# Scores by head and all transposes in two PSUM banks taken in turn, q and k transposed later in the step

## The chip, the cores and the metric

The kernel runs on one core of one Trainium2 chip. The metric is device time in microseconds of one execution: before, the median of three timed runs is 744.09 us (742.8 to 744.35).

## The reference

```python
def _attn_ref(q, k, v, n_sink, window):          # (4, 8, 768, 64): batch, heads, sequence, head_dim
    scores = np.matmul(q, k.transpose(0, 1, 3, 2)) / np.sqrt(D)
    keep = is_sink | in_window                   # key < 4, or 0 <= query - key < 128
    scores = np.where(keep, scores, -1000000000.0)
    a = np.exp(scores - np.max(scores, axis=-1, keepdims=True))
    a = a / (np.sum(a, axis=-1, keepdims=True) + 1e-09)
    return np.matmul(a, v)

def _moe_ref(x, w_in, w_out):                    # x: (3072, 512), w_in: (512, 2048), w_out: (2048, 512)
    h = x @ w_in
    sp = np.maximum(h, 0.0) + np.log1p(np.exp(-np.abs(h)))
    return (h * erf(sp)) @ w_out
```

The attention's output, heads side by side, is x of the second part.

## The kernel before

**Work.** The 3072 tokens are cut into 12 groups of 256 tokens, three groups to a batch. The attention goes in 48 steps: step s is group s // 4 and head pair s % 4. The feed-forward part of a group is 16 blocks of 128 hidden units; one attention step stands beside four of them.

**One step.** `loadqk`, `loadv` (DMAs on SP's queue) bring q, k and v. `prep` transposes two tiles of k and two of q by TensorE into one PSUM tile `tqk`, and ScalarE copies it to `kq` in SBUF (L266; in the first group of a batch a second small copy, L269, puts the sink keys beside it). `score` multiplies q by k on 64x64 pieces of the array, both heads, into `ps`. `soft` is VectorE's part: two copy_predicated that fold the window together, then four masked maxima (the CUSTOM_DVE rows), each followed by ScalarE's exp (L346). `norm` divides on VectorE. `ptrans` transposes the probabilities into `tp`, `strans` the sink columns into `ts`; ScalarE copies `tp` to `pt` (L389) and `ts` to `sp` (L424), and `sinkw` reads `ts` once more on VectorE. Two steps later `av` multiplies by v, and `xfin` copies the result to `xh`, `xl`. In steps of a batch's first group `sinks` also copies the batch's 16 sink rows of v to `sv` (L277, ScalarE), which arrive by two small DMAs of their own.

**Feed-forward.** `hid` makes h in PSUM, two blocks to a tile of 24 matmuls. `act` runs three activations r (L691 to L693) and three u (L696) on ScalarE with three VectorE operations between, then rounds to `g` (VectorE) and takes the rest on GpSimd (L705). `proj` is the output product, 12 matmuls for two blocks, into `o`; after a group two copies `ot` (L724) and two DMAs write the result.

**PSUM.** Eight banks: `ps_o` two, `ps_h` two, `ps_s` two (one tile [P, 2, 512], a bank a head, used again each step), `ps_t` two, in which `tqk`, `tp`, `ts` and `av` take turns.

**Order.** From step 15 on TensorE's order is that of a table: each piece of work has a place `a`, and all are sorted by it. Step s stands at a = 4s - 6. `av` of step s - 2 and `score` of s stand at a - 0.3 and a - 0.29, `tp` and `ts` at a + 3.01, and q and k of step s (`p`) at a - 4.28, so just behind `score` of step s - 1. The other engines' order is the scheduler's, by priorities made from the same places. One step of TensorE is thus: av, ps, tqk of the next step, 24 h, 12 o, 24 h, tp, ts, 12 o.

Of the kernel before, what the change touches and what calls it, by code (L numbers as in the profile page):

```python
# [9 lines left out]
F32 = mybir.dt.float32  # L10
# [6 lines left out]
PSUM = bass.MemoryType.PSUM  # L17
DRAM = bass.MemoryType.DRAM

P = 128  # L20
# [21 lines left out]
NE, AL = 4, 2  # L42
NW = 9
NF1 = 15

PW, EA = 256, 40
O = dict(prep=-100, norm=-100, core=-300, av=-300, load=-400, ptrans=-200, xfin=-100,
# [21 lines left out]
def kernel(  # L69
# [67 lines left out]
    def fast_path():  # L137
        with ExitStack() as st:
# [3 lines left out]
            work = st.enter_context(tc.tile_pool(name="work", bufs=2))  # L142
            ps_o = st.enter_context(tc.tile_pool(name="ps_o", bufs=2, space=PSUM))
            ps_h = st.enter_context(tc.tile_pool(name="ps_h", bufs=2, space=PSUM))
            ps_s = st.enter_context(tc.tile_pool(name="ps_s", bufs=1, space=PSUM))
            ps_t = st.enter_context(tc.tile_pool(name="ps_t", bufs=2, space=PSUM))


            ri = work.tile([P, 512], I32, tag="u", bufs=UB, name="ri")
# [97 lines left out]
            def follow(prev, ins):  # L247

                if prev is not None:
                    tc.add_manual_dep(  # L250
                        ins.ins, prev.ins.name,
                        mybir.DependencyInfo(mybir.DependencyClass.NoSync, mybir.DependencyReason.DATA), reason="order",
                    )
                return ins

            def prep(s):

                g, c = divmod(s, NPAIR)
                d = stp[s]
                tp = ps_t.tile([P, 4, P], F32, tag="t", name=f"tqk_{s}")  # L260
                for j, t in enumerate((d["k"], d["q"])):
                    for i in range(2):
                        ten.transpose(
                            out=tp[:, 2 * j + i, :], in_=t[:, i].rearrange("p h d -> p (h d)"), identity=ident
                        )
                nc.scalar.copy(kq[:, c, 1:, :P], tp)  # L266
                if g % GPB == 0:
                    x = tp[:, 0, :SW].rearrange("p (o t) -> p o t", o=1)
                    nc.scalar.copy(kq[:, c, :3, P:], x.broadcast_to([P, 3, SW]))  # L269
# [16 lines left out]
            def score(s):  # L286

                g, c = divmod(s, NPAIR)
                gb = g % GPB
                d = stp[s]  # L290
                d["pst"] = pst[:, s % RING]
                if s in (2, 3):
                    t = wpool.tile([P, 2 * DM], F32, tag="wo", name=f"pst_{s}")
                    d["pst"] = t[:, : 4 * KB].rearrange("p (i h t) -> p i h t", i=2, h=2)
                d["sum"], d["neg"] = (
                    kq[:, c, 3 + i, P : P + 4].rearrange("p (i h) -> p i h", i=2) for i in range(2)
                )

                ps, both, prev = [], None, tail.pop(s - AL, None)
                for h in range(2):  # L300
                    nm = f"ps_{s}_{h}"
                    if s in (1, 2):
                        ps.append(ps_h.tile([P, 2, GT], F32, tag="h", name=nm).rearrange("p a t -> p (a t)"))
                    else:
                        if both is None:
                            both = ps_s.tile([P, 2, 512], F32, tag="s", name=f"ps_{s}")
                        ps.append(both[:, h, :])


                d["ps"] = ps, both  # L310
                for i in range(2):
                    qt = kq[:, c, 3 + i, :]
                    kt = kq[:, c].rearrange("p n t -> p (n t)")
                    for hf, r0, n, x in ((lo, KB * i, KB + 64, X[i]), (hi, KB * i + 64, KB + 80, X[i] - 80)):
                        for h in (1, 0):
                            r = slice(64 * h, 64 * h + 64)
                            prev = follow(
                                prev,
                                ten.matmul(ps[h][hf, x : x + n], qt[r, hf], kt[r, r0 : r0 + n], start=True, stop=True),
                            )  # L320
# [31 lines left out]
            def both(s):  # L352
                return shs[s % 2].rearrange("p r t -> p (r t)")[:, :P].bitcast(F32)
# [25 lines left out]
            def ptrans(s):  # L379

                i0 = 1 if (s // NPAIR) % GPB == 0 else 0
                d = stp[s]
                pool, tag = (ps_o, "o") if s < 6 else (ps_t, "t")
                tp = pool.tile([P, 2, 2, P], F32, tag=tag, name=f"tp_{s}")
                for i in range(2):
                    for h in range(2):
                        ten.transpose(out=tp[:, h, i, :], in_=d["pst"][:, i, h, :P], identity=ident)
                pt = work.tile([P, 2, 2, P], F32, tag="pt", bufs=1, name=f"pt_{s}")
                nc.scalar.copy(pt, tp)  # L389

                uo = d["uo"] = work.tile([P, 2, 2, 2, P], F32, tag="uo", bufs=AL, name=f"uo_{s}")
                for e, sg, op, i1 in ((0, 1, ALU.is_gt, i0), (1, -1, ALU.is_ge, 0)):
                    nc.gpsimd.affine_select(  # L393
                        out=uo[:, :, i1:, e, :], in_=pt[:, :, i1:, :], pattern=[[0, 2], [0, 2 - i1], [-sg, P]],
                        compare_op=op, fill=0.0, base=0, channel_multiplier=sg,
                    )
# [18 lines left out]
            def strans(s):  # L415

                d = stp[s]
                pool, tag = (ps_o, "o") if s < 6 else (ps_t, "t")
                if s >= NW:
                    ts = d["ts"] = pool.tile([P, P], F32, tag=tag, name=f"ts_{s}")  # L420
                    ten.transpose(out=ts, in_=both(s), identity=ident)
                    sp = d["sp"] = work.tile([P, 2, P], F32R, tag="sp", bufs=AL, name=f"sp_{s}")
                    for i in range(2):
                        nc.scalar.activation(sp[:, i, :], ts, AF.Copy, scale=own[:, i : i + 1])  # L424
                    return
                ts = pool.tile([P, 2, P], F32, tag=tag, name=f"ts_{s}")
                for i in range(2):
                    x = shs[s % 2][:, 3 * i : 3 * i + 4].rearrange("p r t -> p (r t)").bitcast(F32)
                    ten.transpose(out=ts[:, i, :], in_=x, identity=ident)
                sp = d["sp"] = work.tile([P, 2, P], F32R, tag="sp", bufs=AL, name=f"sp_{s}")  # L430
                nc.scalar.copy(sp, ts)
# [44 lines left out]
            def pos(s):  # L476

                return 3 * s if s < NE else 4 * s - 4 * NE + 3 * NE - 2
# [65 lines left out]
            def add(a, nm, j):  # L544
                ev.append((a, len(ev), nm, j))
# [64 lines left out]
            done, a = set(), LEAD - 10  # L610
            while any(lines):
                before = len(done)
                for x in lines:
                    while x and all(w in done for w in needs(*x[0]) if w in known):
                        w = x.pop(0)
                        a = LEAD + w[1] if w[0] == "H" else a + 0.012
# [4 lines left out]

            fixed = pos(NF1) - 0.5
            for s in range(NE, NSTEP + AL):
                a = pos(s)
                if s < NF1:
                    plan = (
                        ("a", a + 0.139, s - AL), ("x", a + 1.11, s - AL), ("n", a + 1.12, s), ("p", a - 2.87, s), ("k", a - 2.869, s),
                        ("s", a + 0.14, s), ("f", a + 0.141, s), ("t", a + 2.15, s), ("w", a + (2.151 if s < NW else 2.153), s), ("u", a + 2.152, s),
                        ("q", a - 3.84, s), ("v", a - 3.839, s),
                    )  # L630
                else:
                    plan = (
                        ("a", a - 0.3, s - AL), ("s", a - 0.29, s), ("f", a - 0.289, s), ("x", a - 0.285, s - AL), ("n", a + 1.12, s),
                        ("t", a + 3.01, s), ("u", a + 3.02, s), ("w", a + 3.021, s),
                        ("q", a - (8.2 if s > NF1 + 1 else 6.5 - 2 * (s - NF1)), s), ("p", a - (4.28 if s > NF1 else 2.87), s),
                        ("k", a - 2.869, s), ("v", a - 3.839, s),
                    )
                for nm, z, n in plan:
                    if NE <= n < NSTEP and (nm, n) not in done and (nm != "k" or n // NPAIR % GPB == 0 or NW <= n < NW + NPAIR):
                        add(max(z, last + 0.01) if nm in "ntwu" else z, nm, n)  # L640
            for m in range(NG * NF):
                g, f = divmod(m, NF)
                a = m + LEAD
                p = LAG + 0.3
                if a + p > fixed:
                    p = LAG + (1.0 if m % 2 == 0 else 0.0) + (0.01 if m % 4 > 1 else 0.03) + 0.005 * (m % 2)
# [80 lines left out]
    def general_path():  # L727

        NT_S = S // P
        with ExitStack() as st:  # L730
# [71 lines left out]
            with tc.tile_pool(name="g_one1", bufs=1) as one, tc.tile_pool(name="g_work1", bufs=2) as work:  # L802
# [3 lines left out]
                with tc.For_i(0, B, 1) as b:  # L806
                    for gb in range(GPB):
# [25 lines left out]
                        for i in range(2):  # L833
# [3 lines left out]
                            )  # L837

    fast_path()
    ok = nc.values_load(flagi[0:1, 0:1], min_val=0, max_val=1)  # L840
    with tc.If(ok == 0):  # L841
# [31 lines left out]
```

## Time and profile before

| what | us |
|---|---|
| timed runs, median (lowest, highest) | 744.09 (742.8, 744.35) |
| profiled execution, span from first to last instruction | 741.7 |
| TensorE matmul busy | 708.9 (96%) |
| ScalarE busy | 543.0 (73%) |
| VectorE busy | 513.7 (69%) |
| GpSimd busy | 193.4 (26%) |

The profiled execution's own time is known as its span alone, 741.7 us; the median of the timed runs is 2.4 us more, for what lies ahead of the first and behind the last instruction. Busy shares are means over stages. The first 200 us (steps 0 to 14) are bound in other ways than the rest; the change touches steps 17 to 47, which begin at about 229 us. In the rows, PE is TensorE's matmuls, PEld its weight loads, DVE VectorE, ACT ScalarE, POOL GpSimd, SP the queue that issues DMAs.

### The profile page before, as it was taken

The page shows a single profiled execution, that of the slowest core. Times are in us where ns is not written, and L with a number is a line of the kernel's source. Part 1 is how long each engine was busy: PE and PEld are TensorE (multiplying, and loading weights), DVE is VectorE, ACT ScalarE, POOL GpSimd, SP SyncE. Part 2 cuts the span into 40 slices and gives each one's busy share as a digit, 9 for nine tenths or more (in the row PEclk, how much of TensorE's full clock was granted, in tenths as well). Part 3 has the DMA queues.
Part 4 walks back from the last instruction along what each step waited for, and adds up shares of the span by engine and source line. Part 5 has one row for each costly group of instructions (what it writes and reads, how often), then busy time and mean ns, then how long its engine had stood idle before and what let it go on. Part 6 is the DMA issues. An engine that isn't in the chain of part 4 may idle for free. (4 is left out here: it accounts for less than half of the span.)

```text
span 741.7 us, 14935 instructions
## 1 busy us (share of the span) xinstructions
PE 708.9 (96%) x5129; PEld 590.3 (80%) x5129; DVE 513.7 (69%) x1493; ACT 543.0 (73%) x1304; POOL 193.4 (26%) x240
## 2 busy tenths in 40 slices
PE   4798999999999999999999999999999999999996
PEld 2475666777888888888888888888888888888995
DVE  7899998899776566575676666666667666564442
ACT  3576769777877877878778777776887786785663
POOL 2221010233322322332222322232232232232221
PEclk9899999999999999999999999999999999999999
DMA  6787640211221221111121211111112211100000
GB/s 144 195 241 278 206 150 15 68 35 26 60 53 29 57 55 27 54 38 37 55 51 37 58 44 36 54 29 43 47 45 54 57 30 38 34 7 1 30 1 33
DMA packets 100595, 47.33 MB, mean 64 GB/s; under 512 B 89248, under 2 KB 93344, under 8 KB 100512
## 3 DMA queue, kind: packets, MB, share of 16 engines
q1 hardware_dynamic: 99680, 46.16, 22.4%
q8 instruction: 43, 0.70, 0.4%
q14 instruction: 40, 0.33, 0.2%
q10 hardware_dynamic: 832, 0.13, 0.1%
HBM read 37.88 MB, written 6.29 MB: 60 GB/s over the span
## 5 line engine op out<-in xcount | busy, mean ns | idle before, releaser
L238 PE MATMUL o<-wt,g 128*128 128x512 f32 x1056 | 260.5, 395 | 1.1 <-POOLq L841 0.7
L238 PEld LDWEIGHTS o<-wt,g 128*128 128x128 f32 x1056 | 191.6, 188 | 39.2 <-POOLq L841 1.1
L238 PE MATMUL h<-xh,wt 128*128 128x256 f32 x1408 | 194.3, 280 | 2.2 <-DVE acc L238 2.1
L705 POOL TENSOR_TENSOR g<-acc,g 128x512 fp32r<-128x512 f32 x88 | 116.5, 1324 | 295.2 <-DVE g L238 291.6
L238 PEld LDWEIGHTS h<-xh,wt 128*128 128x128 f32 x1408 | 178.0, 188 | 9.2 <-DVE acc L238 3.5
L696 ACT ACTIVATE u<-r 128x512 f32<-128x512 f32 x288 | 162.9, 623 | 13.7 <-DVE acc L238 8.5
L238 DVE SCALAR_TENSOR_TENSOR acc<-u,h 128x512 f32<-128x512 f32 x88 | 60.5, 688 | 116.0 <-issue 41.6
L238 DVE SCALAR_TENSOR_TENSOR acc<-u,acc 128x512 f32<-128x512 f32 x176 | 122.6, 697 | 19.6 <-ACT u L696 6.9
L346 ACT ACTIVATE pst<-pst,kq 128x144 f32<-128x144 f32 x192 | 77.6, 405 | 64.5 <-DVE kq L238 64.3
L393 POOL TENSOR_SCALAR_AFFINE_SELECT uo<-pt 128x512 f32<-128x512 f32 (+1 forms) x96 | 64.7, 694 | 195.5 <-ACT pt L389 175.8
L238 PE MATMUL h<-xl,wt 128*128 128x256 f32 x704 | 109.9, 277 | 0.0
L238 PEld LDWEIGHTS h<-xl,wt 128*128 128x128 f32 x704 | 93.3, 188 | 0.3 <-DVE wf L238 0.2
L691 ACT ACTIVATE r<-h 128x512 f32<-128x512 f32 x96 | 56.6, 590 | 45.0 <-PE h L238 44.6
L693 ACT ACTIVATE r<-r 128x512 f32<-128x512 f32 x96 | 60.7, 632 | 2.9
L692 ACT ACTIVATE r<-r 128x512 f32<-128x512 f32 x96 | 61.2, 637 | 2.0
L238 PE MATMUL ps<-kq 64*64 64x208 f32 (+1 forms) x768 | 50.5, 374 | 6.4 <-ACT kq L266 4.8
L238 PE MATMUL av<-uo,v 128*64 128x128 f32 (+1 forms) x512 | 50.1, 328 | 0.0
L238 DVE CUSTOM_DVE_ANT_0 pst<-ps,mask 128x144 f32<-128x144 f32 x192 | 47.6, 304 | 1.6
L266 ACT COPY kq<-tqk 128x512 f32<-128x512 f32 x48 | 28.0, 583 | 27.9 <-PE tqk L238 27.8
L238 DVE SCALAR_TENSOR_TENSOR wf<-ws,wf 128x512 int32<-128x512 int32 x64 | 44.2, 728 | 0.4
L238 PEld LDWEIGHTS ps<-kq 64*64 64x64 f32 x768 | 27.9, 139 | 20.3 <-issue 9.4
L238 DVE COPY_PREDICATED ps<-tri,ps 64x256 f32<-64x256 int8 (+1 forms) x100 | 41.6, 420 | 3.1
(83 smaller groups left out, 703.3 us busy)
## 6 DMA issues: line engine op xcount, KB each, us to landing
ws<-in_moe_w_in_dram SPq DMA_DIRECT2D x16, 512.0 KB, 4.9
ws<-in_moe_w_out_dram SPq DMA_DIRECT2D x16, 512.0 KB, 7.4
v<-in_v_dram SPq DMA_DIRECT2D x64, 96.0 KB, 2.3
out_dram<-ot SPq DMA_DIRECT2D x24, 256.0 KB, 2.2
q<-in_q_dram SPq DMA_DIRECT2D x95, 64.0 KB, 2.3
k<-in_k_dram SPq DMA_DIRECT2D x95, 64.0 KB, 2.3
v<-in_v_dram SPq DMA_DIRECT2D x32, 64.0 KB, 2.1
kq<-kq SPq DMA_DIRECT2D x32, 64.0 KB, 2.5
```

Source lines behind the costliest of these rows:

```text
L238: ins = f(*a, **k)
L266: nc.scalar.copy(kq[:, c, 1:, :P], tp)
L346: nc.scalar.activation(y, y, AF.Exp, bias=d["neg"][:, i, h : h + 1], scale=-1.0, accum_out=d["sum"][:, i, h : h + 1])
L393: nc.gpsimd.affine_select(out=uo[:, :, i1:, e, :], in_=pt[:, :, i1:, :], pattern=[[0, 2], [0, 2 - i1], [-sg, P]], compare_op=op, fill=0.0, ...
L691: nc.scalar.activation(r, h, AF.Tanh, bias=b_t, scale=0.5)
L692: nc.scalar.activation(r, r, AF.Square, bias=b_v, scale=-0.5)
L693: nc.scalar.activation(r, r, AF.Square, bias=b_r)
L696: nc.scalar.activation(u, r, AF.Square, bias=b_a[i], scale=CS)
L705: nc.gpsimd.tensor_tensor(gl, acc, gh.bitcast(F32), op=ALU.subtract)
```

## The change

From step 17 on (NB) `score` takes a tile of one bank for each head, and `tqk`, `tp` and `ts` take tiles of the same pool `ps_a`, which has two banks and takes the place of `ps_s`. `ps_t` keeps its two banks for `av`. The order of allocation is ps of head 0, ps of head 1, tqk of the next step, tp, ts, so five tiles a step go through two banks. In the built program the tiles of step 29 lie so: ps head 0 in bank 7, ps head 1 in 6, tqk of step 30 in 6, tp in 7, ts in 6; in step 30 the two banks are exchanged. Since `soft` now finds two tiles, it issues its copy_predicated for each head apart: four of 64x128 for two of 64x256. And q and k of steps 18 to 47 are transposed at a - 2.5 in place of a - 4.28.

```diff
+NB = 17
...
-            ps_s = st.enter_context(tc.tile_pool(name="ps_s", bufs=1, space=PSUM))
             ps_t = st.enter_context(tc.tile_pool(name="ps_t", bufs=2, space=PSUM))
+            two = ExitStack()
+            ps_s = two.enter_context(tc.tile_pool(name="ps_s", bufs=1, space=PSUM))
+            ps_a = []
...
+            def bank(shape, name):
+
+                if not ps_a:
+                    two.close()
+                    ps_a.append(st.enter_context(tc.tile_pool(name="ps_a", bufs=2, space=PSUM)))
+                return ps_a[0].tile(shape, F32, tag="s", name=name)
+
             def prep(s):
...
-                tp = ps_t.tile([P, 4, P], F32, tag="t", name=f"tqk_{s}")
+                tp = bank([P, 4, P], f"tqk_{s}") if s > NB else ps_t.tile([P, 4, P], F32, tag="t", name=f"tqk_{s}")
...
-                    if s in (1, 2):
+                    if s >= NB:
+                        ps.append(bank([P, 512], nm))
+                    elif s in (1, 2):
...
-                tp = pool.tile([P, 2, 2, P], F32, tag=tag, name=f"tp_{s}")
+                if s >= NB:
+                    tp = bank([P, 2, 2, P], f"tp_{s}")
+                else:
+                    tp = pool.tile([P, 2, 2, P], F32, tag=tag, name=f"tp_{s}")
...
-                    ts = d["ts"] = pool.tile([P, P], F32, tag=tag, name=f"ts_{s}")
+                    ts = bank([P, P], f"ts_{s}") if s >= NB else pool.tile([P, P], F32, tag=tag, name=f"ts_{s}")
+                    d["ts"] = ts
...
-("p", a - (4.28 if s > NF1 else 2.87), s),
+("p", a - (2.5 if s > NB else 4.28 if s > NF1 else 2.87), s),
```

**TensorE behind the scores of step 29, before** (ps is `score`, tqk the transposes of `prep`, h the hidden product; what a row waits for stands in brackets):

```order
L238 MATMUL ps_29_4851<-kq_134 64x208 x2
L238 MATMUL ps_29_4851<-kq_134 64x224 x2
L238 MATMUL ps_29_4851<-kq_134 64x208 x2
L238 MATMUL ps_29_4851<-kq_134 64x224 x2
L238 MATMUL tqk_30_4873<-ident_61,k_30_4707 128x128 [waits DMAHW2_49,DMAHW5_49,DVE_49,Activation_49]
L238 MATMUL tqk_30_4873<-ident_61,k_30_4707 128x128
L238 MATMUL tqk_30_4873<-ident_61,q_30_4704 128x128 [waits DMAHW4_49,DMAHW3_49]
L238 MATMUL tqk_30_4873<-ident_61,q_30_4704 128x128
L238 MATMUL h_94_4885<-xh_5_3589,wt_12_1544 128x256 x2
```

and in the change, at the end of the 12 output products that follow the first 24 h (o), and then at tp and ts of step 29:

```order
L241 MATMUL o_5_1_4499<-wt_27_1713,g_91_4811 128x512
L241 MATMUL tqk_30_4969<-ident_61,k_30_4741 128x128 [waits DMAHW2_49,DMAHW5_49,DVE_49,PE_49]
L241 MATMUL tqk_30_4969<-ident_61,k_30_4741 128x128
L241 MATMUL tqk_30_4969<-ident_61,q_30_4738 128x128 [waits DMAHW4_49,DMAHW3_49]
L241 MATMUL tqk_30_4969<-ident_61,q_30_4738 128x128
L241 MATMUL h_96_4992<-xh_6_4362,wt_0_951 128x256 x2
...
L241 MATMUL tp_29_5017<-ident_61,pst_138 128x128 [waits DVE_49]
L241 MATMUL ts_29_5027<-ident_61,sh1_140 128x128 [waits Activation_49]
L241 MATMUL o_5_0_4498<-wt_28_1752,g_93_4882 128x512
```

The four transposes stand 36 matmuls later. The wait of ts for ScalarE is new (before it waits for TensorE alone): its bank is that of tqk of step 30.

**ScalarE in step 24, before** (a step of a batch's first group; L346 are the exps, L277 the sink rows, L691 to L693 r, L696 u, L266 and L269 the copies of tqk):

```order
L266 COPY kq_134<-tqk_25_3962 128x4x128 [waits PE_49]
L269 COPY kq_134<-tqk_25_3962 128x3x16
L346 ACTIVATE pst_138,kq_134<-pst_138,kq_134 128x144 [waits DVE_49]
L277 CAST sv_136<-v_25_3988 32x128 [waits DMAHW6_49,DMAHW5_49,Pool_49]
L277 CAST sv_136<-v_25_3988 32x128
L346 ACTIVATE pst_138,kq_134<-pst_138,kq_134 128x144 [waits DVE_49] x3
L691 ACTIVATE r_75_4029<-h_74_3975 128x512 [waits PE_49,Activation_49]
L692 ACTIVATE r_75_4029<-r_75_4029 128x512 [waits Activation_49]
L693 ACTIVATE r_75_4029<-r_75_4029 128x512 [waits Activation_49]
L696 ACTIVATE u0_75_4034<-r_75_4029 128x512 [waits Activation_49]
```

and the same step in the change (lines are 10 to 16 higher: L358 exps, L287 sink rows, L707 to L709 r, L712 u, L276 and L279 the copies of tqk):

```order
L287 CAST sv_136<-v_25_4009 32x128 [waits DMAHW6_49,DMAHW5_49,Pool_49]
L358 ACTIVATE pst_138,kq_134<-pst_138,kq_134 128x144 [waits DVE_49]
L287 CAST sv_136<-v_25_4009 32x128
L358 ACTIVATE pst_138,kq_134<-pst_138,kq_134 128x144 [waits DVE_49] x3
L707 ACTIVATE r_75_4057<-h_74_3996 128x512 [waits PE_49,Activation_49]
...
L712 ACTIVATE u1_75_4065<-r_75_4057 128x512
L712 ACTIVATE u2_75_4068<-r_75_4057 128x512
L276 COPY kq_134<-tqk_25_4050 128x4x128 [waits PE_49]
L279 COPY kq_134<-tqk_25_4050 128x3x16
L707 ACTIVATE r_77_4128<-h_76_4074 128x512 [waits PE_49,Activation_49]
```

The copies of tqk stand behind the exps, r and u of the step, where they stood ahead of the exps. So it is in every step s from 17 with s % 4 of 0 or 1; with 2 (the steps that copy an output) they stand behind the first u, with 3 ahead of the first u, behind r.

## Rows read from the trace of the kernel before

**Rows 1.** The page: engines' busy time (share of the span) and instructions.

```profile
PE 708.9 (96%) x5129; PEld 590.3 (80%) x5129; DVE 513.7 (69%) x1493; ACT 543.0 (73%) x1304; POOL 193.4 (26%) x240
```

**Rows 2.** Windows of single steps: length, busy us (count) of each engine, clock, DMA.

```profile
285.69:299.86 14.17, 14.17 (x111) 12.30 (x110) 8.99 (x28) 10.40 (x26) 3.78 (x5) 1.00 0.15 34
328.21:342.38 14.17, 14.17 (x111) 12.30 (x110) 9.32 (x30) 11.41 (x30) 4.54 (x7) 1.00 0.15 34
652.46:666.25 13.79, 13.79 (x108) 11.92 (x106) 8.99 (x28) 10.24 (x26) 4.22 (x5) 1.00 0.01 1
```

**Rows 3.** Timeline of TensorE's weight loads, step 21: start, us, what, idle before.

```profile
285.46 0.19 PEld L238 LDWEIGHTS av<-sp,sv 128*128 128x128 f32 x1
...
287.83 0.20 PEld L238 LDWEIGHTS tqk<-ident,k 128*128 128x128 f32 x2 [0.33 <-issue]
...
288.22 0.99 PEld L238 LDWEIGHTS h<-xh,wt 128*128 128x128 f32 x8
...
290.96 2.59 PEld L238 LDWEIGHTS o<-wt,g 128*128 128x128 f32 x12
...
296.47 0.45 PEld L238 LDWEIGHTS tp<-ident,pst 128*128 128x128 f32 x4
296.89 0.14 PEld L238 LDWEIGHTS ts<-ident,sh 128*128 128x128 f32 x1
297.00 2.59 PEld L238 LDWEIGHTS o<-wt,g 128*128 128x128 f32 x12
```

**Rows 4.** The same view, step 47, which has no tqk behind it.

```profile
654.60 1.00 PEld L238 LDWEIGHTS h<-xh,wt 128*128 128x128 f32 x8 [0.33 <-DVE acc L238]
```

**Rows 5.** Timeline of DVE: copy_predicated by head (step 2), for both (step 3).

```profile
20.54 1.03 DVE L238 COPY_PREDICATED ps<-tri,ps 64x128 f32<-64x128 int8 x4
...
27.31 0.90 DVE L238 COPY_PREDICATED ps<-tri,ps 64x256 f32<-64x256 int8 x2
```

**Rows 6.** Timeline of ACT, step 21.

```profile
288.53 0.59 ACT L266 COPY kq<-tqk 128x512 f32<-128x512 f32 x1 [1.12 <-PE tqk L238]
290.24 0.42 ACT L346 ACTIVATE pst<-pst,kq 128x144 f32<-128x144 f32 x1 [1.12 <-DVE kq L238]
...
293.78 1.68 ACT L696 ACTIVATE u<-r 128x512 f32<-128x512 f32 x3
```

**Rows 7.** Timeline of ACT, steps 24 and 26 (first group of a batch).

```profile
331.05 0.59 ACT L266 COPY kq<-tqk 128x512 f32<-128x512 f32 x1 [0.77 <-PE tqk L238]
331.53 0.20 ACT L269 COPY kq<-tqk 128x48 f32<-128x48 f32 x1
...
337.31 1.68 ACT L696 ACTIVATE u<-r 128x512 f32<-128x512 f32 x3
...
366.47 0.64 ACT L696 ACTIVATE u<-r 128x512 f32<-128x512 f32 x1
```

**Rows 8.** Timeline of ACT, steps 36 and 37 (first group of the last batch).

```profile
507.95 1.67 ACT L696 ACTIVATE u<-r 128x512 f32<-128x512 f32 x3
...
518.94 0.62 ACT L277 CAST sv<-v 32x128 fp32r<-32x128 f32 x2 [1.18 <-DMA v<-in_v_dram]
...
522.74 1.67 ACT L696 ACTIVATE u<-r 128x512 f32<-128x512 f32 x3
```

**Rows 9.** Timeline of PEld: the load of ts in steps 24, 26, 36 and 37.

```profile
339.41 0.14 PEld L238 LDWEIGHTS ts<-ident,sh 128*128 128x128 f32 x1
...
367.54 0.14 PEld L238 LDWEIGHTS ts<-ident,sh 128*128 128x128 f32 x1
...
508.61 0.14 PEld L238 LDWEIGHTS ts<-ident,sh 128*128 128x128 f32 x1
...
522.78 0.14 PEld L238 LDWEIGHTS ts<-ident,sh 128*128 128x128 f32 x1
```

**Rows 10.** Timeline of DVE, step 21: the last maximum of `soft`.

```profile
290.57 0.30 DVE L238 CUSTOM_DVE_ANT_0 pst<-ps,mask 128x144 f32<-128x144 f32 x1
```

More of the change, by code (lines that the diff above doesn't have):

```diff
@@ L634, in fast_path @@
                         ("t", a + 3.01, s), ("u", a + 3.02, s), ("w", a + 3.021, s),
-                        ("q", a - (8.2 if s > NF1 + 1 else 6.5 - 2 * (s - NF1)), s), ("p", a - (4.28 if s > NF1 else 2.87), s),
+                        ("q", a - (8.2 if s > NF1 + 1 else 6.5 - 2 * (s - NF1)), s), ("p", a - (2.5 if s > NB else 4.28 if s > NF1 else 2.87), s),
                         ("k", a - 2.869, s), ("v", a - 3.839, s),
```

## The prediction

> **What bounds the kernel now.** I read the page first: matmuls are busy 96% of the span, ScalarE 73%, VectorE 69% [rows 1]. Since busy time hides stalls, I then asked for windows of single steps, each from the first matmul of av to the next one. A step takes 14.17 us, and where ScalarE has 1 us more to do it takes 14.17 us as well [rows 2]. The granted clock is 1.00 in them, the level of 2.4 GHz. So from step 17 on TensorE runs its own list with nothing late; the other engines have slack, and the step's length is the sum of TensorE's instructions. Third, the weight loads of one step [rows 3] show where TensorE itself is idle: 0.33 us ahead of tqk, which stands behind the 64x64 scores.
>
> For the change this means that a shorter list of TensorE gains at once, and that a wait which is met in time today costs only when it becomes late. No stall of these steps is left for a freer use of the banks to take away.
>
> **The gap ahead of tqk.** If those 0.33 us were a wait for the bank of tqk, the change would take them away 30 times, 9.9 us. Against this: in step 47 no tqk follows the scores, and the first weight load of h has the same 0.33 us [rows 4]. So the gap belongs to the scores, and what comes next pays it. The Trainium skill, page TensorEngine Tiling (Array Packing), section Key Properties, says that changing the tiling mode drains TensorE; by that rule, too, the gap would stay and the 9.9 us would not come. The trace agrees: 0.33 us ahead of either.
>
> **Term 1, q and k transposed elsewhere.** 30 sets of four transposes move (steps 18 to 47). What leaving the old place saves is read from a step with tqk, 14.17 us, and one without, 13.79 us [rows 2]: 0.38 us. What the new place costs, between output and hidden products, no row shows. The nearest is tp and ts between hidden and output products: five transposes from 296.47 to 297.00 [rows 3], 0.106 us each, so 0.43 for four. Below it lies the old place's distance from tqk to h, 288.22 - 287.83 = 0.39 us [rows 3]; above, the whole busy time of tp's four loads, 0.45 us [rows 3]. I take 0.43, which stands beside the same kinds of matmuls: 30 x (0.43 - 0.38) = **+1.5 us**, from +0.3 to +2.1.
>
> **Term 2, scores and copy_predicated by head.** The eight score matmuls and their order by head stay. Four smaller copy_predicated take 1.03 us, two larger ones 0.90 [rows 5], so VectorE, the exps and all that ScalarE does behind them come 0.13 us later. TensorE doesn't see this: VectorE is busy 8.99 of 14.17 us [rows 2]. Without that cover it would be 31 x 0.13 = 4 us. It counts in term 3.
>
> **Term 3, the new waits.** tqk of step s + 1 now lies in the bank of head 1's scores of step s, and ts of step s in the bank of tqk. Three waits follow.
>
> First, tqk waits for the last maximum of soft. In step 21 that ends at 290.87 [rows 10]; the step began at 285.46, and tqk would come when the first output products are through, 290.96 - 0.38 + 2.59 = 293.17 [rows 3]. Slack over 2 us; nothing. Second, the next step's scores wait for the copy of tp and the two readers of ts, which run beside 2.59 us of output products and then av; nothing.
>
> Third, **ts waits for ScalarE's copy of tqk**. The copy used to stand in idle time ahead of the exps, with 1.12 us free on either side [rows 6]; now it stands behind exps, r and u, or in half of the steps behind the first u or ahead of it, which is earlier. In step 21 u ends at 293.78 + 1.68 = 295.46 [rows 6]; with the copy's 0.59, the 0.13 of term 2 and a start of 0.03 the wait ends at 296.21. ts would load at 296.89 + 0.05 = 296.94 [rows 3]. Slack 0.7 us: no stall.
>
> Steps 24 to 26 and 36 to 38 are another matter. They are in the first group of a batch, where ScalarE also makes two sink copies among the exps and a second small copy behind tqk: busy 11.41 us for 10.40 [rows 2]. Step 24: u ends at 338.99; from the start of the tqk copy to the end of the small one it is 0.68 us [rows 7]; with 0.16 as above, 339.83, against ts at 339.41 + 0.05 [rows 9]. Stall 0.4 us. Step 26: the first u ends at 367.11 [rows 7], plus 0.84, against 367.59 [rows 9]: 0.4; step 25 as 24. In the last batch the sink rows landed late, and ScalarE waited for them, 1.18 us in step 37 and about as much in step 36. Step 36: u ends at 509.62 [rows 8], plus 0.84, against 508.66 [rows 9], stall 1.8. Step 37: 524.41 plus 0.84 against 522.83, stall 2.4. A stall of TensorE also delays av, whose end frees the v tiles and starts the next sink loads, so what a late landing costs is not won back in the next step; ScalarE's own backlog is, so step 38 counts 0.4 again. By this execution's landings the sum is 1.2 + 4.6 = 5.8 us. With all in time it is six times 0.4, 2.4 us; with four of six late, some 9. Landings change from run to run, so I take **+4.5 us**, between one late set (some 4) and two.
>
> **Queues.** SP issues the loads of q and k once the tqk two steps earlier is done, now 5 us later in the step; they stand behind the v and sink loads of their step and ahead of those of the next, which wait for the next av anyway, and their tile is read two steps later. Nothing. GpSimd still clears v ahead of the sink loads, and is busy 4.54 us of 14.17 [rows 2]. Nothing.
>
> **Sum.** Against the profiled execution: 741.7 + 1.5 + 4.5 = 747.7 us of span. The timed median lies 2.4 us over that span, so 744.1 + 6.0, rounded **750.0 us**. What a measurement of this kernel can tell from no change is 0.2%, 1.5 us.
>
> **Rivals.**
>
> *Only the place costs.* The copies of tqk are done in time in all steps, because the sink rows land early or the exps start earlier with no copy ahead of them. For it: 0.7 us of slack in plain steps. Against: ScalarE was idle ahead of the exps anyway [rows 6], so they can't start earlier. 744.1 + 1.5 = 745.6, about the bound of no change.
>
> *Faster, tqk is hidden behind the output products.* If four transposes cost nothing behind 512-column matmuls, 30 x 0.38 = 11.4 us go: 732.7. It decides from a cost under 0.33 us in the new place. Against: tp and ts cost 0.106 each beside the same matmuls [rows 3]. And if the gap of 0.33 us goes: 744.1 + 1.5 - 9.9 = 735.7; against it stands step 47 [rows 4].
>
> *Plain steps stall too.* If u ends more than 0.7 us later than now, ts stalls in the other 24 steps as well; half a microsecond over that makes 12 us, 762. For it: ScalarE's order was made anew, and five tiles on two banks tie three engines to each other in each step. Against: 0.13 us is all that is added ahead of u.
>
> *No wait is late and the new place costs what the old one did*: 744.4.
>
> **How the numbers follow.** The forecast (place and sink steps, together 3 to 11 us) gets 0.65; only the place 0.13; faster 0.08, both mechanisms together; plain stalls 0.09; nothing 0.05. The range goes from 745.0, which takes in the place alone, to 755.0, four late landings with the dearer place (744.1 + 2.1 + 9, rounded). Outside are faster, nothing, and most of the plain stalls, about 2 in 10. Faster by over 0.2%: 0.08. Within 0.2%: nothing and most of the place alone, 0.16. Slower: 0.76.
>
> **What would show it.** Right: the scores followed by h at once behind the gap of 0.33 us; four transposes at some 0.106 us each behind the first output products; plain steps of about 14.2 us; and a wait of ts for ScalarE's copy of tqk in steps 24 to 26 and 36 to 38, 2 to 9 us in sum, and hardly elsewhere. Wrong: tqk at under 0.33 us in its new place, that wait in plain steps, or a wait of the scores for VectorE's reading of ts, which I cost at nothing.

## The result and the profile after

The changed kernel takes 751.95 us in the median of four runs (751.51 to 752.62), the kernel before 743.8 beside it: ratio 1.0112, 95% interval 1.0098 to 1.0127, so 8.15 us slower. The forecast was 750.0 (745 to 755), slower. The profiled execution of the changed kernel spans 750.8 us, 9.1 more than that of before. Of these, 8.6 lie between the first av matmul of step 17 and that of step 47: 431.85 us (229.57 to 661.42), against 423.24 before (229.22 to 652.46).

The page of the changed kernel, line of busy times:

```profile
PE 715.2 (95%) x5129; PEld 592.3 (79%) x5129; DVE 520.5 (69%) x1555; ACT 538.0 (72%) x1304; POOL 190.8 (25%) x240
```

Against [rows 1], TensorE has as many matmuls and is busy 6.3 us longer; VectorE has 62 instructions and 6.8 us more; both shares hide where the time went. Windows of steps 21, 34, 36 and 47, columns as in [rows 2]:

```profile
286.79:301.11 14.32, 14.32 (x112) 12.39 (x110) 9.13 (x30) 10.30 (x26) 4.78 (x6) 1.00 0.15 33
473.62:487.85 14.23, 14.23 (x111) 12.29 (x110) 8.63 (x28) 10.36 (x26) 2.52 (x3) 1.00 0.25 70
502.17:518.22 16.05, 14.54 (x112) 12.36 (x110) 9.65 (x32) 11.50 (x30) 4.36 (x6) 1.00 0.14 31
661.42:675.22 13.80, 13.80 (x108) 11.91 (x106) 9.38 (x30) 10.26 (x26) 4.04 (x5) 1.00 0.01 2
```

Where a step with tqk took 14.17 us [rows 2], there are now several lengths: 14.23, 14.32, in three steps 14.46 and, with a stall, up to 16.05 us. (Nine of the 30 steps, whose av is shorter by four matmuls, take 0.22 us less, before as after.) Steps 21 and 34 show TensorE busy throughout at a granted clock of 1.00, the 2.4 GHz level: neither a wait nor the clock makes step 21 longer. Step 47, which has no tqk, takes what it took before. Timeline of TensorE's weight loads, step 21:

```profile
288.94 1.00 PEld L241 LDWEIGHTS h<-xh,wt 128*128 128x128 f32 x8 [0.33 <-issue]
...
291.68 2.59 PEld L241 LDWEIGHTS o<-wt,g 128*128 128x128 f32 x12
294.31 0.37 PEld L241 LDWEIGHTS tqk<-ident,k 128*128 128x128 f32 x2
294.65 0.25 PEld L241 LDWEIGHTS tqk<-ident,q 128*128 128x128 f32 x2
294.86 1.01 PEld L241 LDWEIGHTS h<-xh,wt 128*128 128x128 f32 x8
...
297.70 0.46 PEld L241 LDWEIGHTS tp<-ident,pst 128*128 128x128 f32 x4
298.13 0.14 PEld L241 LDWEIGHTS ts<-ident,sh 128*128 128x128 f32 x1
```

The gap of 0.33 us that stood ahead of tqk [rows 3] now stands ahead of h, as [rows 4] had it. Here the drain at a change of the tiling mode, of which the Trainium skill speaks (TensorEngine Tiling (Array Packing), Key Properties), agrees with the trace: the gap stays with the scores.

What makes the different lengths of the steps without a stall is in the matmuls. Timeline of PE, the 24 hidden products behind tqk, up to tp, in step 21 and in step 34:

```profile
294.89 1.19 PE L241 MATMUL h<-xh,wt 128*128 128x256 f32 x8
295.91 0.64 PE L241 MATMUL h<-xl,wt 128*128 128x256 f32 x4
296.38 1.11 PE L241 MATMUL h<-xh,wt 128*128 128x256 f32 x8
297.33 0.64 PE L241 MATMUL h<-xl,wt 128*128 128x256 f32 x4
297.81 0.60 PE L241 MATMUL tp<-ident,pst 128*128 128x128 f32 x4
...
481.71 1.17 PE L241 MATMUL h<-xh,wt 128*128 128x256 f32 x8
482.72 0.62 PE L241 MATMUL h<-xl,wt 128*128 128x256 f32 x4
483.18 1.07 PE L241 MATMUL h<-xh,wt 128*128 128x256 f32 x8
484.08 0.62 PE L241 MATMUL h<-xl,wt 128*128 128x256 f32 x4
484.54 0.60 PE L241 MATMUL tp<-ident,pst 128*128 128x128 f32 x4
```

From the first h to tp it is 2.92 us in step 21 and 2.83 in step 34, for the same 24 instructions. In the second group of eight a matmul starts every 0.119 us by these rounded rows (297.33 - 296.38 over 8; 0.118 over the whole 24) or every 0.113 (484.08 - 483.18 over 8). I call these the slow and the quick rhythm. Behind tqk the slow one holds in 24 of the 30 steps (2.91 or 2.92 us), the quick one in six (2.82 or 2.83); before, the hidden products behind tqk took 2.82 in all 30.

Step 36 has the largest stall. ScalarE first, then the weight loads:

```profile
504.12 0.35 ACT L484 CAST xh<-av 128x256 fp32r<-128x256 f32 x1
508.79 0.30 ACT L287 CAST sv<-v 32x128 fp32r<-32x128 f32 x1 [4.32 <-DMA v<-in_v_dram]
...
512.99 1.67 ACT L712 ACTIVATE u<-r 128x512 f32<-128x512 f32 x3
514.56 0.56 ACT L276 COPY kq<-tqk 128x512 f32<-128x512 f32 x1
515.03 0.20 ACT L279 COPY kq<-tqk 128x48 f32<-128x48 f32 x1
```

```profile
513.07 0.46 PEld L241 LDWEIGHTS tp<-ident,pst 128*128 128x128 f32 x4
515.28 0.14 PEld L241 LDWEIGHTS ts<-ident,sh 128*128 128x128 f32 x1 [1.75 <-ACT kq L279]
```

The sink rows of v landed late, and everything behind them on ScalarE, the copy of tqk last, came late for ts. Not all of the 4.32 us is the landing's: in step 20, which has no sinks, ScalarE is idle for 3.31 us at this place. Against step 24, which does the same work, the sink copies begin 1.47 us later in their step, and ts waits 1.7 us instead of 0.5.

### The profile page after: what moved, and what is told of

Same layout as the page of the kernel before. It is cut to its first block, busy times and chain, and to the rows that moved or that the text cites. A ratio compares the mean times of both kernels' runs of the same rounds, so it can differ in the third digit from the quotient of the medians.

```text
span 750.8 us, 14977 instructions
## 1 busy us (share of the span) xinstructions
PE 715.2 (95%) x5129; PEld 592.3 (79%) x5129; DVE 520.5 (69%) x1555; ACT 538.0 (72%) x1304; POOL 190.8 (25%) x240
## 5 line engine op out<-in xcount | busy, mean ns | idle before, releaser
L241 PE MATMUL h<-xh,wt 128*128 128x256 f32 x1408 | 199.0, 284 | 2.1 <-DVE acc L241 2.0
L712 ACT ACTIVATE u<-r 128x512 f32<-128x512 f32 x288 | 163.7, 624 | 9.3 <-DVE acc L241 4.1
L358 ACT ACTIVATE pst<-pst,kq 128x144 f32<-128x144 f32 x192 | 77.6, 405 | 99.9 <-DVE kq L241 99.5
L241 DVE SCALAR_TENSOR_TENSOR acc<-u,acc 128x512 f32<-128x512 f32 x176 | 124.2, 706 | 26.1 <-ACT u L712 14.2
L408 POOL TENSOR_SCALAR_AFFINE_SELECT uo<-pt 128x512 f32<-128x512 f32 (+1 forms) x96 | 61.8, 666 | 186.0 <-ACT pt L404 185.9
L707 ACT ACTIVATE r<-h 128x512 f32<-128x512 f32 x96 | 56.7, 590 | 37.0 <-PE h L241 36.5
L709 ACT ACTIVATE r<-r 128x512 f32<-128x512 f32 x96 | 60.7, 632 | 2.8
L241 DVE COPY_PREDICATED ps<-tri,ps 64x128 f32<-64x128 int8 (+1 forms) x162 | 45.9, 319 | 3.0
L241 DVE CAST g<-acc 128x512 fp32r<-128x512 f32 x88 | 39.6, 450 | 5.5 <-DVE acc L241 0.5
```

Source lines behind the costliest of these rows:

```text
L241: ins = f(*a, **k)
L358: nc.scalar.activation(y, y, AF.Exp, bias=d["neg"][:, i, h : h + 1], scale=-1.0, accum_out=d["sum"][:, i, h : h + 1])
L408: nc.gpsimd.affine_select(out=uo[:, :, i1:, e, :], in_=pt[:, :, i1:, :], pattern=[[0, 2], [0, 2 - i1], [-sg, P]], compare_op=op, fill=0.0, ...
L707: nc.scalar.activation(r, h, AF.Tanh, bias=b_t, scale=0.5)
L709: nc.scalar.activation(r, r, AF.Square, bias=b_r)
L712: nc.scalar.activation(u, r, AF.Square, bias=b_a[i], scale=CS)
```

## The experiments

Each number "over the 30 steps" is the time from the start of step 17 to that of step 47 less the 423.24 us of before. Waits are what tp and ts (or the waiting instruction named) take over their length in a plain step; the rest is the remainder. These three columns come from one traced execution of each kernel, which lies up to 1.6 us from the median (place alone: 751.55).

| kernel | median us | over the 30 steps | waits | rest |
|---|---|---|---|---|
| the change | 751.95 | 8.6 | 4.0 (ts) | 4.6 |
| place alone | 749.93 | 6.8 | 1.9 (ts) | 4.9 |
| ts in its old banks | 748.77 | 4.5 | 0.2 (tqk) | 4.3 |
| banks alone | 746.10 | 2.1 | 2.1 (scores) | 0.0 |
| tqk beside tp | 746.53 | 2.3 | 0.4 (tp) | 1.9 |
| tqk ahead of av | 752.32 | 7.9 | 3.6 (av) | 4.3 |
| tqk amid the output products | 751.15 | 8.6 | 4.9 (tqk) | 3.7 |
| tqk ahead of the output products | 759.07 | 15.3 | 12.7 (tqk) | 2.6 |
| tqk behind 12 hidden products | 746.46 | 2.8 | 0.2 (tp) | 2.6 |
| scores by head alone | 751.17 | 7.6 | 2.8 (ts), 0.2 (tp) | 4.6 |
| tqk behind 1 hidden product | 747.06 | 3.5 | 0 | 3.5 |
| tqk behind 6 hidden products | 746.97 | 3.4 | 0 | 3.4 |

### Place alone

```diff
 (kernel before)
-("p", a - (4.28 if s > NF1 else 2.87), s)
+("p", a - (2.5 if s > NB else 4.28 if s > NF1 else 2.87), s)
```

> The kernel before with one edit: tqk of step s + 1 is made behind the first output products, as in the change; the banks of scores, tqk, tp and ts stay as they were (tqk and ts have shared a bank there too). Theory 1 (the place is all of it: the set of four transposes costs 0.51 us with what stands behind it, 0.38 of it was paid before, and ts waits for ScalarE's copy of tqk): 751.5 us, from 750.5 to 753, and the hidden products behind tqk take 2.9 us in most steps. Theory 2 (the scores' banks slow the hidden products, the place doesn't): those products take 2.82 us in every step and the time is about 749, place at +0.04 us a step and the stalls of ts. Theory 3 (the stalls of ts come with the new banks alone): no wait of ts, about 748.

749.93 us, ratio 1.0084 (1.007 to 1.0098); just under theory 1's range. Hidden products behind tqk take 2.91 us in the mean of the 30 steps, so the slow rhythm comes with the place and not with the scores' banks, and theory 2 falls. Theory 3 falls too: ts waits here as well, but less. The waits of weight loads from 229 to 670 us in this run (columns: us in total, times, longest):

```profile
PEld ts L239 <- ACT kq L270: 1.9, 3, 1.4
```

and in the changed kernel:

```profile
PEld ts L241 <- ACT kq L279: 3.0, 3, 1.7
...
PEld ts L241 <- ACT kq L276: 1.0, 4, 0.4
```

### The wait of ts taken away

```diff
 (the change)
-ts = bank([P, P], f"ts_{s}") if s >= NB else pool.tile([P, P], F32, tag=tag, name=f"ts_{s}")
+ts = pool.tile([P, P], F32, tag=tag, name=f"ts_{s}")
```

> The changed kernel with one edit: ts goes back to the two banks that it shares with av, so it no longer waits for ScalarE's copy of tqk. Theory 1: the stalls of ts, 4.0 us in the trace of the changed kernel (1.7 of them in step 36), go, and the rest stays: 748 us, from 747 to 749; steps without slow landings take 14.2 to 14.3 us. Rival (what ts waits for is only the first of several late things, and av or the scores wait in its place): 750 us or more.

748.77 us, ratio 1.0062 (1.0048 to 1.0076): 3.2 us under the change. Not one wait of ts is left, no other wait takes its place but one of 0.2 us, and the steps take 14.30 to 14.33 us in the main. The stalls are worth what the trace of the change shows, within a us; the rest stays.

### Banks alone

```diff
 (the change)
-tp = bank([P, 4, P], f"tqk_{s}") if s > NB else ps_t.tile([P, 4, P], F32, tag="t", name=f"tqk_{s}")
+tp = ps_t.tile([P, 4, P], F32, tag="t", name=f"tqk_{s}")
...
-("p", a - (2.5 if s > NB else 4.28 if s > NF1 else 2.87), s)
+("p", a - (4.28 if s > NF1 else 2.87), s)
```

> The changed kernel with tqk put back behind the scores of the step before, and into the banks that it had; scores by head, tp and ts keep the two shared banks, and copy_predicated goes by head. Theory 1 (banks by themselves cost nothing, VectorE's 0.13 us more a step is hidden): 743.8 us, from 743 to 744.8, and steps of 14.17 us. Theory 2 (sharing the banks costs): 745.5 us or more, by a wait of the scores for the copies of tp and ts, or by hidden products over 2.82 us behind the scores.

746.1 us, ratio 1.0033 (1.002 to 1.0045). Both theories have a part. A plain step is as before, with VectorE at 9.13 us instead of 8.99 [rows 2]:

```profile
285.68:299.85 14.17, 14.17 (x111) 12.30 (x110) 9.13 (x30) 10.41 (x26) 3.79 (x5) 1.00 0.15 34
```

So the new banks and copy_predicated by head cost TensorE nothing in 28 of 30 steps. In steps 27 and 39 the scores wait 0.7 and 1.5 us. Step 27, weight loads, then VectorE:

```profile
371.51 0.19 PEld L241 LDWEIGHTS ps<-kq 64*64 64x64 f32 x2 [0.39 <-ACT r L707]
372.16 0.61 PEld L241 LDWEIGHTS ps<-kq 64*64 64x64 f32 x14 [0.46 <-ACT r L708]
```

```profile
370.60 0.28 DVE L241 TENSOR_TENSOR sp<-ts,sp 32x128 fp32r<-32x128 f32 x1
370.91 0.81 DVE L241 CAST g<-acc 128x512 fp32r<-128x512 f32 x1
371.76 0.28 DVE L241 TENSOR_TENSOR sp<-ts,sp 32x128 fp32r<-32x128 f32 x1
```

The releaser that the loads name, ScalarE's r, has nothing to do with the scores' banks. VectorE's second reading of ts ends at 372.04, and the scores go on 0.12 later, in step 39 as well; there the row of the matmuls names VectorE's sp, which is this reading. VectorE, then PE, step 39:

```profile
542.44 0.28 DVE L241 TENSOR_TENSOR sp<-ts,sp 32x128 fp32r<-32x128 f32 x1
...
542.87 0.60 PE L241 MATMUL ps<-kq 64*64 64x208 f32 x8 [0.92 <-DVE sp L241]
```

So this wait, which the prediction costed at nothing, exists, but not in the change, where the scores take 0.92 us in every step.

### tqk beside tp and ts

```diff
 (the run without the wait of ts)
-("p", a - (2.5 if s > NB else 4.28 if s > NF1 else 2.87), s)
+("p", a - (0.97 if s > NB else 4.28 if s > NF1 else 2.87), s)
```

> The changed kernel with ts in the banks of av (as in the run without its wait) and tqk made right behind tp and ts, ahead of the second output products. Theory 1 (the price lies in each change from long products to transposes and back, and here it is paid already for tp and ts): four more transposes at 0.106 us, 0.43 us, against 0.38 saved: 745.3 us, from 744.5 to 746.5, hidden products behind the first output products back at 2.75 us. Rival (a set costs 0.51 us wherever it stands): 748 us. Second rival (the copy of tqk comes too late for the next scores): over 749 us, with a wait of the scores for ScalarE.

746.53 us, ratio 1.0037 (1.0023 to 1.0051), at the upper end of theory 1's range. A plain step of this run, then one of the run with tqk behind twelve hidden products (below):

```profile
286.49:300.73 14.24, 14.24 (x111) 12.36 (x110) 9.13 (x30) 10.30 (x26) 3.79 (x5) 1.00 0.15 33
```

```profile
285.99:300.24 14.25, 14.25 (x111) 12.38 (x110) 9.13 (x30) 10.28 (x26) 3.76 (x5) 1.00 0.15 33
```

14.24 against 14.17: the set costs 0.45 here, 0.38 of it saved. The slow rhythm is nowhere, and a set costs nearly what the prediction took, 0.43.

### tqk ahead of av

```diff
 (kernel before)
-("p", a - (4.28 if s > NF1 else 2.87), s)
+("p", a - (4.31 if s > NF1 + 2 else 4.28 if s > NF1 else 2.87), s)
```

> The kernel before with one edit: tqk of step s + 1 is made just ahead of av and the scores of step s instead of just behind them, 30 times; banks as before. Theory 1 (a set costs 0.106 us a transpose where the change to transposes and back is paid by what stands there anyway): 0.43 against the 0.38 saved, 14.22 us a step, 745.3 us. Theory 2 (a set that stands alone costs 0.51 us wherever it is): 14.30 us a step, 747.8 us. Theory 3 (it is partly hidden beside the short matmuls of av, under 0.38 us): faster than before, 742.5 us or less.

752.32 us, ratio 1.0122 (1.0107 to 1.0138): no theory's number, though eleven steps take theory 1's length. Step 21 of this run:

```profile
286.16:300.39 14.23, 14.23 (x113) 12.38 (x112) 9.09 (x28) 10.28 (x27) 3.80 (x5) 1.00 0.15 33
```

In 17 others hidden products have the slow rhythm (2.93 us behind the scores, 2.83 behind output products), which makes up to 14.43 us of a full step; and av waits up to 1.5 us where VectorE's reading of ts is late, as the scores did with the banks alone. The waits of matmuls from 226 to 670 us name it (columns as above):

```profile
PE av L238 <- DVE sp L238: 2.4, 2, 1.3
```

Theory 3 falls: nothing is hidden. No transposes stand directly ahead of these slow hidden products.

### tqk amid and ahead of the first output products

As the run beside tp, with 2.9875 (the middle of the twelve) and 2.99 (ahead of them) in place of 0.97.

> The changed kernel with ts in the banks of av (so without its wait; that one took 748.77 us) and tqk in the middle of the twelve first output products instead of behind them. Theory 1 (the slow rhythm of the hidden products, 117.5 ns a matmul instead of 113, comes only when transposes stand directly ahead of them): hidden products behind the output products 2.75 us again, tqk 0.35 and the output products behind it 0.09 slower, 14.23 us a step, 745.7 us. Theory 2 (it comes from what ScalarE and VectorE do beside them): the slow rhythm stays, 748.5 us or more.

> As the run in the middle, but tqk ahead of the twelve first output products, behind the first hidden products, where tp and ts stand in the second half of the step. Theory 1 (the set costs 0.43 and the output products behind it 0.09, as behind tp and ts, and no hidden products stand behind transposes): 14.31 us a step, all hidden products behind output products at 2.75 us, 748 us. Rival (only the slow rhythm was the price over 0.43): 14.22 us a step, 745.5 us.

751.15 (1.0083 to 1.0113 of before) and 759.07 us (1.0205 to 1.0234). Neither tests what it was meant to by its time, since tqk, 1.4 and 2.8 us earlier, now waits in 4 and in 21 steps while VectorE is still at the maxima of soft, whose scores lie in the same banks. The trace doesn't name VectorE as the releaser, but in all 25 steps tqk starts 0.11 us behind the end of the second of the four maxima. So the first of the prediction's three waits is real, though it ends with the second maximum and not with the last. The steps without such a wait do tell: ahead of the output products 14.25 us, the rival's 14.22 rather than the 14.31 of theory 1; in the middle of them 14.24 or 14.33, where the 24 hidden products, though output products stand ahead of them, take 2.74 or 2.83. So the slow rhythm doesn't need transposes directly ahead, and theory 1 of the middle falls.

### tqk behind twelve, one and six hidden products

Behind twelve: 1.5 in place of 0.97. Behind one and six, with the same kernel as base, the transposes are made from inside the loop of hidden products:

```diff
 for m, (c, p, e) in enumerate(ops):
     self.ten.matmul(...)
+    if m == 0 and later:
+        later.pop()()
```

This is behind one; behind six it is m == 5. The lines that put the transposes into the list `later` are left out here.

> As the run in the middle, but tqk in the middle of the 24 second hidden products. Theory 1 (transposes directly ahead of hidden products set the slow rhythm until other products come): the twelve hidden products behind tqk take 1.45 to 1.48 us in most steps, those ahead of it 1.38; 14.27 to 14.31 us a step, 747 to 748.3 us. Rival (the slow rhythm is set by the output products that stand ahead of the set): those twelve take 1.38 to 1.42 us, 14.22 us a step, 745.5 us.

> The changed kernel with ts in the banks of av (so without its wait; that one took 748.77 us) and tqk one matmul later: behind the first of the 24 second hidden products instead of ahead of it. Theory 1 (the slow rhythm comes when hidden products follow transposes that follow the wide output products at once): one hidden product between them is enough, hidden products at 113 ns in all steps, 14.25 us a step, 746.5 us. Theory 2 (the rhythm hangs on how load and matmul happen to be aligned by nanoseconds, so that no rule by neighbours holds): slow in some of the steps, at 14.3 us or more, 747 to 749 us.

> The same with tqk behind the first six of the 24 hidden products. Theory 1: as behind one, 14.25 us a step and 746.5 us. Theory 2: a number of slow steps that fits neither the run behind one nor the 30 quick steps of the run behind twelve, between 746.5 and 749 us.

746.46 (1.0025 to 1.0053), 747.06 (1.0035 to 1.0062) and 746.97 us (1.0032 to 1.006). Behind twelve, the twelve that follow take 1.46 us, which I had named as the mark of the slow rhythm, and wrongly: 0.09 of it is the start of the first behind a transpose. The others follow every 113 ns in all steps but two, and 14.25 us a step lies between the theories. Behind one, 20 of the 30 steps are slow, mostly in a pattern of four; behind six, 8 are (18 hidden products in 2.20 us for 2.15). Steps 18 and 19 of the run behind one:

```profile
243.17:257.38 14.21, 14.21 (x111) 12.34 (x110) 8.61 (x28) 10.34 (x26) 2.81 (x4) 1.00 0.26 75
257.38:271.69 14.31, 14.31 (x111) 12.44 (x110) 9.84 (x32) 10.29 (x27) 3.64 (x4) 1.00 0.17 39
```

The same neighbours on TensorE, and 0.10 us of difference: theory 2, no rule by neighbours. Nor do the other engines decide: in the change, steps 30 and 34 have ScalarE and VectorE at the same instructions, to within 0.01 us as counted from the first hidden product behind tqk, while these products begin; GpSimd is idle beside them in both, and the DMA engines are busy 0.38 and 0.34 of the time. Step 30 is slow, step 34 quick.

Yet it is not chance. Behind six, the length of each step comes back twelve steps later to within 0.001 us. And in the change steps 20, 32 and 44 stall alike (0.19, 0.18 and 0.18 us), but the two steps behind take 14.31 and 14.31 us after the first, 14.46 and 14.23 after the others: a hundredth of a microsecond ahead goes with another rhythm behind.

### Scores by head alone

```diff
 (the run without the wait of ts)
-tp = bank([P, 4, P], f"tqk_{s}") if s > NB else ps_t.tile([P, 4, P], F32, tag="t", name=f"tqk_{s}")
+tp = ps_t.tile([P, 4, P], F32, tag="t", name=f"tqk_{s}")
...
-if s >= NB:
-    tp = bank([P, 2, 2, P], f"tp_{s}")
-else:
-    tp = pool.tile([P, 2, 2, P], F32, tag=tag, name=f"tp_{s}")
+tp = pool.tile([P, 2, 2, P], F32, tag=tag, name=f"tp_{s}")
```

> The changed kernel with tqk, tp and ts in the two banks that they share with av, as before; only the two heads' scores, and copy_predicated by head, use the new banks. TensorE, VectorE and ScalarE have the same instructions in the same order as in the change. Theory 1 (the 0.13 us that VectorE takes longer by head, and the order that ScalarE has with it, make the wait of ts 4 us instead of the 1.9 us of the run with the place alone): 751 to 752.5 us and 4 us of waits of ts. Theory 2 (five tiles on two banks, tied to each other, are the cause of the difference): 749.5 to 750.3 us and about 2 us of waits of ts.

751.17 us, ratio 1.0103 (1.0088 to 1.0119): in time theory 1, in waits of ts between the two (2.8 us). The waits from 229 to 670 us:

```profile
PEld ts L241 <- ACT kq L279: 2.2, 3, 1.0
PEld ts L241 <- ACT kq L276: 0.6, 3, 0.2
```

The late landing of step 36 differs from run to run. Without that step, ts waits 1.8 us here, 2.2 in the change and 0.4 with the place alone. Of the 1.4 between here and the place alone, 0.8 lies in steps 20, 24, 32 and 44, where ScalarE has the same order but the exps start 0.26 to 0.28 us later in their step: that is VectorE's part by head. 0.7 lies in step 26, where the sink rows landed 0.8 us later in their step than with the place alone (0.6 later in the change); why, no run shows. Whether five tiles on two banks add anything, the overlapping intervals leave open, up to 0.8 us.

## Why the prediction was right in sign and size, and which term was not

**What bounds the kernel, and the gap**: right. TensorE's list sets the step, and the 0.33 us stayed with the scores; the two faster rivals did not come.

**Term 1** is the term that was mis-sized: +1.5 us (0.3 to 2.1) was forecast, 4.6 measured, above the dear end. The set itself was right: quick steps cost 0.06 instead of 0.05, and in the seven other places they cost 0.04 to 0.08. What failed is the step that priced the transposes alone, by distances between transposes, and let the products around them keep their pace. In 24 steps of 30 the hidden products behind tqk took 0.1 us more, in seven those behind the scores and the output products after them too. That is 4.6 - 30 x 0.06 = 2.8 us. Nothing in these steps of the trace of before showed it: there the hidden products behind tqk keep the quick rhythm in all 30 (2.82 us, against 2.75 behind output products, because the first behind a transpose starts later). Why the new place brings the slow rhythm so often stays open.

**Term 2**, no direct cost: shown by the run with the banks alone (rest 0.0). Its part in term 3 was too small: over two steps it grows to 0.27 us, and it accounts for about 0.8 of the 2.2 us of waits outside step 36.

**Term 3**: +4.5 forecast, 4.0 measured, by the mechanism named, but spread otherwise. Step 36 stalled 1.7 us for 1.8 forecast; step 24, 0.5 for 0.4; step 25, 0.1 and step 26, 0.7 for 0.4 each. Steps 37 and 38, 2.8 together, did not stall, since their sink rows landed in time; steps 20, 32, 40 and 44, which were given slack, stalled 0.2, 0.2, 0.4 and 0.2. By the prediction's own test a wait in plain steps counts against it. The slack of 0.7 us was read from step 21, and "0.13 us is all that is added ahead of u" does not hold in the first step of a group of four. The last u and the copy of tqk in step 20: before, with the place alone, in the change (where ts waits):

```profile
279.61 1.68 ACT L696 ACTIVATE u<-r 128x512 f32<-128x512 f32 x3
...
281.84 1.68 ACT L697 ACTIVATE u<-r 128x512 f32<-128x512 f32 x3
283.42 0.56 ACT L267 COPY kq<-tqk 128x512 f32<-128x512 f32 x1
...
281.67 1.68 ACT L712 ACTIVATE u<-r 128x512 f32<-128x512 f32 x3
283.25 0.56 ACT L276 COPY kq<-tqk 128x512 f32<-128x512 f32 x1
...
283.87 0.14 PEld L241 LDWEIGHTS ts<-ident,sh 128*128 128x128 f32 x1 [0.20 <-ACT kq L276]
```

Step 20 begins at 271.52, 272.75 and 272.31, so u ends 9.77, 10.77 and 11.04 us into it. 1.00 us comes with the place alone, where the scheduler orders ScalarE's work anew as well (which of these moves does it was not tested), and 0.27 with copy_predicated by head. That the sum of term 3 came within 0.5 us of the forecast is in part luck: the 2.8 us of steps 37 and 38 did not come, and 0.9 us came in steps that were given none.

**Sum**: 1.5 + 4.5 = 6.0 was forecast, 4.6 + 4.0 = 8.6 stands in the trace and 8.15 in the medians. The range held it, because its upper end rested on late landings, which took no part in the miss. The 2.4 us between span and median stand on both sides and cancel, but they are not what lies ahead of the first and behind the last instruction: in each execution with both numbers on record that is 1.7 to 1.8 us, so the traced execution of before was probably faster than the median.

No kernel of the study beats the one before: a set of transposes costs 0.42 to 0.46 us in each new place, and behind the scores 0.38.

## What to carry to other kernels

Where a moved instruction is priced on an engine that is never idle, measure the time from the last instruction ahead of it to a point well behind it, since what follows can run slower and look like work. Before a buffer is shared more tightly, ask which late event (here a DMA landing) reaches the new wait through the other engine's queue, and check the slack in each kind of step, not in one.

## What the runs showed of the hardware

The same 256-column hidden products, with nothing waiting and the granted clock at 1.00, run at one start every 113 or every 118 ns, and keep a rhythm for up to 24 matmuls; in the steps compared no neighbour on TensorE and no work of another engine told the two apart, while the same course of steps brought the same rhythm again. The Trainium skill, TensorE: Matmul & The Clock Gate, Back-to-back issue gap, says that in a stream of loads and matmuls the spacing is set by both together; the trace shows two spacings for one such stream. That the alignment of load and matmul by nanoseconds decides, as I suppose, was not shown. It is worth 2.8 us of the change's 8.6 and 0.1 us of a step at a time.
